# 48 rows for the half tiles, and a new order of the first thousand tasks, in a fused RWKV-7 and MLP kernel

## The chip, the core and the metric

The kernel runs on one core of a Trainium2 chip. A core has a matrix engine (TensorE, PE in the profile, with its weight loads as PEld), a vector engine (VectorE, DVE), a scalar engine (ScalarE, ACT), a general engine (GpSimd, POOL) and a queue engine (SyncE, SP), which here issues every DMA. The engines run side by side, each takes its instructions strictly in order, and semaphores make one wait for another. Matrix products land in PSUM, which has eight banks; everything else lies in SBUF, 128 partitions wide.

The metric is device time in microseconds (us), the median of several executions. Before the change it is 678.03 us (three runs, 677.79 to 678.33).

## The reference

Two stages follow each other. The first is a recurrence over 768 time steps, for 4 batches and 8 heads of size 40:

```python
for t in range(S):
    kt, vt, rt = (k[:, :, t], v[:, :, t], r[:, :, t])
    wt, at, bt = (w[:, :, t], a[:, :, t], b[:, :, t])
    y[:, :, t] = np.einsum('bhd,bhde->bhe', rt, state)
    Sa = np.einsum('bhde,bhe->bhd', state, at)
    state_decay = state * wt[:, :, None, :] - np.einsum('bhd,bhe->bhde', Sa, bt)
    state = state_decay + np.einsum('bhd,bhe->bhde', vt, kt)
```

The second takes y as 3072 tokens of 320 numbers through an MLP: `h = x @ w_in` (320 to 2048), `g = h / (1 + exp(-1.702 h))`, `g @ w_out` (2048 to 320). All is float32.

## The kernel before

**Units and chunks.** The sequence is cut into 12 chunks of 64 steps, and each chunk into two units (two batches each), so there are 24 units, numbered 0 to 23. Inside a unit the recurrence is solved as a triangular system: products between the inputs (`ps_A`, `ps_RV`, `ps_N`), an inverse in five levels of block doubling (`ps_level`), two corner products (`ps_Q`, `ps_T`), the solve (`ps_X`), and the reading of y and of the new state (`ps_y`). Units of the same parity follow each other through the state: `ps_zT` and `ps_rz` bring the state of unit i - 2 into unit i. When both units of a chunk are done, the chunk goes through the MLP: 80 tasks `ps_up`, in eight groups, and after the activation 32 products per group of tokens, `ps_down`.

**The loads (function `load`, line 495).** Per unit five inputs come from DRAM: `ak` (the inputs a and k), `b`, `rv` (r and v), `RV` (v again, in another layout) and `time`. `ak`, `b` and `rv` hold two halves of 64 partitions each, one per half of the heads. A head has 40 channels, so of the 64 partitions of a half only the first 40 carry data. The array in DRAM has all 128 rows, with zeros in the others. The kernel fetches 40 rows of each half, with one DMA per half; the remaining partitions of `ak` and `b` are set to zero once, at the start. `ak` and `rv` have 4 KB per row, `b` 2 KB. Each of these tiles has two buffers, so the load for unit i waits until unit i - 2 has done with its own.

**The weights (function `weight`).** They arrive packed in eight pieces, numbered 0 to 3 for `w_in` and 4 to 7 for `w_out`, in four DMAs of 320 KB each (task name `wt`). Each piece is then unpacked: one step on ACT (`rebased`, line 447), three on DVE (`bounded`, line 451; `shifted`, line 455; `rounded`, line 459) and one on GpSimd (`joined`, line 463).

**One unit's way to y.** `ak` is multiplied on DVE or GpSimd by decay factors (`ahT`, `khT`, lines 619 and 624), `b` on DVE (line 621). `ps_N` needs both. Its masked copy (line 722, into the tile PT) and the transpose of that (line 729, into EX) feed the first level. In the first four units a level is one product of 64x96 blocks and one with an identity; after each, line 792 copies 768 elements per partition from PSUM into PT, and line 729 transposes 512 of them into EX. The next level needs both. The last level's transpose is ES (line 708). Then come `ps_Q`, line 824 or 826 (QT), `ps_T`, line 838 (T), `ps_X`, line 915 (M), `ps_y`, line 953 (y's read-out), and line 961, which makes x from y. x is stored to DRAM and fetched back in another layout (lines 971 and the one after it); both units of a chunk must be back before its first `ps_up`.

**The order.** The work consists of 2700 tasks. `Plan.add` collects them with what each reads, writes and may run on. No scheduler runs in the kernel: the string `ORDER` lists all tasks in the order in which they are issued, each as a number, a letter for its engine (p PE, a ACT, d DVE, g POOL, s SP) and, for tasks that touch PSUM, the number of the pair of banks (0 to 3). So `108a0` is task 108 on ACT with pair 0. `Plan.listed` reads the string, and the tasks are issued one after the other; an engine executes its own in that order.

Of the kernel before, what the change touches and what calls it, by code (L numbers as in the profile page):

```python
# [107 lines left out]
0s 5s 7s 8s 9s 3a 6s 87p0 88p1 24s 89a1 1s 2s 12s 102a 95d 100p2 90a0 93d 158a 101d2 98p3 96g 10s 94d 17s 97g 16s 99d3 103p1  # L108
4a 11s 132p0 104a1 105d1 142p2 26s 143p3 133a0 106d 130p1 14s 144a3 13s 107p0 15s 18s 151g 108a0 109d0 51s 131a1 110p3 27s
149g 150d 111a3 112d3 159p0 156p1 145a2 161d0 160a0 152g 113p3 345s 92a 162d 25s 153d 114a3 163p2 42s 115d3 34s 19a 274s 264p0  # L110
165d2 265p3 164a2 22d 266a3 166p2 20d 273s 21d 33s 43s 167a2 154p3 168d2 23g 35s 28a 157d1 116p2 155d3 169p1 117a2 118d2 267a0
279d 63s 280g 119p3 277s 171d1 36s 44s 120d3 343s 125d3 278g 124d3 29d 126p2 170a1 123a3 30d 172p1 122a3 127a2 121a 31d 128p2
54s 173a1 287a 288p0 289a0 129d2 32g 174d1 134p3 147s 37a 290d0 175p2 135d3 180a2 146s 178a2 275s 176d2 136p1 179a2 479s 38d
181a2 45s 39d 177a 282g 291d 91s 138a1 182p0 188p3 281d 183a0 186p2 139d 137a1 283p0 187a2 184p1 189a3 40d 276s 292p2 46a
284d0 41g 285p3 185d1 344s 148a 286d3 190p0 293a2 294d2 334p1 335p3 357a 140s 191d0 268g 336a3 315d 192p2 47d 337a1 348d 316p0
194a2 295p3 349d 61s 317a0 195g 60s 347s 358p1 296a3 62s 297d3 360d1 318a0 298p3 271a 361d 319p0 338g 300d3 196s 193a2 320a0
346s 355p2 385d 270s 48d 299a3 362p0 356d2 351g 301p3 363a0 364d0 350g 269s 141s 386p2 197s 302d3 365p0 387a2 352g 359a1 303d3
388a2 323p1 367d0 366a0 321p3 49d 324a1 304p2 322a3 478s 325d1 50g 353p0 309a2 470p3 354d0 209p1 307a2 210p1 310a2 305d2 211p1
308a2 272d 198p0 341a 199p0 72s 212p1 70s 64a 200p0 340s 368p2 52s 342d 339s 69s 201p0 369a2 202p0 370d2 203p0 471a 213p1 65d
214p1 389p2 66d 472a3 483g 204p0 390a2 560s 371p3 67d 306a 53s 215p1 71s 482s 216p1 372a3 217p1 476a 220p2 373d3 68g 218p1  # L120
221p2 477d 219a1 205p0 222p2 206p0 223p2 224p2 207p0 55a 311p3 225p2 79s 312d3 80s 226p2 208a0 58d 313p1 374p3 314d1 227p2 56d
379a3 228p2 229p2 57d 326p0 230a2 59g 393p1 327d0 378a3 391p2 394a1 375d3 231p0 558s 392d2 376a 232p0 233p0 395d1 559s 81s 73a
78s 234p0 480s 381p2 235p0 328p1 481s 382a2 74d 377a3 485d 380a3 236p0 75d 492a 242p2 486d 243p2 82a 76d 484d 77g 383p3 237p0
384d3 244p2 329d1 330d1 488p3 473d 238p0 531d 245p2 487g 246p2 489d3 85d 532p1 239p0 533a1 396p3 331d 332s 474s 475s 534a1
240p0 247p2 397d3 562s 241a0 535p1 83d 490p3 536a1 84d 398p0 572a 491d3 86g 550p1 555s 561s 253p3 399d0 551a 333s 400d0 254p3
401d 402s 554s 255p3 552a1 564d 493p0 705s 556a 567g 570p1 403s 494d0 248p2 563d 566g 249p2 495d0 498d 256p3 571d1 565g 250a2
496a0 251d2 252s 696p1 497g 557d 539p0 537p2 704s 257p3 538a2 540d0 258p3 553d 611d 697a 499d 573p2 784s 700s 259p3 576a2
574d2 710d 260p3 541d0 575d2 404p0 578d 261a3 577g 405p0 579d 698a1 568p2 711g 500p1 406p0 569d2 501a1 407p0 262d3 263s 708s
580p2 702a 502d1 408p0 582d2 409p0 503d 410p0 583d 504a 612p3 411p0 584g 613d3 412p0 614d3 413p0 505p1 709d 414a0 426p3 506d1
427p3 428p3 507d1 429p3 699d 581d2 430p3 615p1 785s 706s 701s 703d 431p3 616a1 585p0 432p3 508d 586a0 433p3 587d0 434p3 509a  # L130
588d 435p3 589d 448p2 436a3 510p1 590p0 511a1 449p2 592d0 591a0 512d1 415p3 513d 416p3 593d 514a 417p3 594g 418p3 515p0 419p3
516a0 517d0 595p1 518d 420p3 596a1 597d1 421p3 598d 422p3 519a 599d 423p3 424p3 520p0 425a3 437p1 521d0 438p1 523d0 522g 439p1
524d0 440p1 525d0 441p1 442p1 526d0 527p3 718p0 929s 528a3 443p1 719d0 787s 444p1 720d0 529p3 445p1 721d0 446p1 530d3 600p0
723d 447a1 542p3 722d 724g 603d0 605a0 619p1 604d0 543d3 450p2 620a1 606d0 544p3 621d1 601d0 602d 617p1 707s 546d3 451p2 618a1
783s 712d 547g 713d 607p0 725p1 608a0 452p2 609p0 453p2 548s 610d0 932s 454p2 727d1 726d1 622p0 728d 545d3 729a 775p1 455p2
623d0 780s 776a 549s 756d 730p3 624p0 456d2 457d2 731d3 458s 459p2 777a1 778g 732d3 786s 788g 781a 779s 626d0 460p2 625d0 627g
733d 795p1 835d 734a 461p2 735p3 791g 462p2 628s 736a3 796d1 737d3 716p0 792g 738d 463p2 782d 739g 1011s 920p1 757p3 925s
464p2 717d0 758a3 629s 759a3 790d 465p2 740p0 789d 466p2 741a0 742d0 921a 797p3 467d2 760p0 1008s 468d2 800a3 923d 652p2 469s
761d0 922a1 653p2 926a 930s 798d3 714p1 799d3 654p2 924s 802d 801g 655p2 934d 803a 656p2 836p0 657p2 715d1 658p2 659p2 837d0
762p3 838d0 927d 660p2 763a3 661p2 764p1 662a2 743d 630p0 744d 928s 631p0 632p0 765d1 804p3 766d1 633p0 805a3 806d3 634p0 807d  # L140
635p0 808a 745p2 636p0 748d2 637p0 749d2 839p1 933g 750d2 638p0 840a1 1009s 751d2 639p0 809p3 746d2 935g 640a0 641p1 810d3
642p1 793p2 747a 811d3 674p0 812d 794d2 813a 752p3 643p1 753a3 814p2 644p1 815a2 816d2 754p3 645p1 755d3 646p1 817d 647p1 818a
767p2 841p3 768d2 648p1 842a3 649p1 819p2 650p1 820a2 821d2 675p0 769p3 822d 651a1 823d 771d3 931s 770d3 772g 824p2 936d 676p0
827a2 828a2 942p1 829a2 677p0 1153s 830a2 937d 945a1 773s 663p3 825d2 664p3 943d1 1156s 826a 665p3 944d1 999p2 947d 946g 666p3
1000a 1004s 980d 940p1 948g 667p3 941d1 668p3 774s 669p3 670p3 831p1 671p3 1001a2 1002d 1003s 832d1 672p3 1005a 1013d 678p0
673a3 1006d 833p2 843p1 679p0 834d2 1007s 844d1 938p2 845d1 680p0 939d2 846p3 681p0 847d3 949p1 1012g 682d0 848p2 950a1 683d0
1014d 684s 685p3 849d2 1015g 1010s 850d2 1021p0 1016g 951d1 686p3 1024a0 1232s 851d 1235s 981p2 687p3 982a2 952d 852s 1022d0
983a2 953g 1144p1 1023d0 688p3 1026d 1145a 1149s 1025d 1027g 984p2 1059d 689p3 1154s 954p0 853s 985a2 1147g 690p3 1158d 1148s
955a0 956d0 986p2 1146a1 957d 1150a 691p3 958d 987a2 1151d 988p0 692p3 989a0 1152s 990d0 959p1 693a3 865p2 960a1 694d3 866p2
961d1 867p2 695s 962d 868p2 963d 1028p0 869p2 1029a0 1030d0 870p2 1031d 1157g 871p2 1159d 1032a 1060p3 872p2 873p2 1061a3  # L150
874p2 1062d3 1033p1 875a2 854p0 1035d1 855p0 1036d 856p0 1037d 1063p3 857p0 1064d3 1034a1 858p0 964p2 859p0 965a2 966d2 1038p1
967d 860p0 1039a1 1040d1 861p0 1041d 1017p3 968a 1042g 862p0 1018d3 863p0 969p2 864a0 876p1 970d2 877p1 972d2 971g 1043p3
973d2 878p1 1044a3 974d2 879p1 975d2 880p1 881p1 1045d3 1019p0 1046d 976p2 1047a 882p1 1020d0 1233s 883p1 977a2 1166p3 884p1
1169a3 1167d3 1377s 978p0 885p1 1168d3 898p2 1171d 1170g 886a1 979d0 887p3 1172a 1048p0 991p1 1051a0 888p3 1052a0 992d1 889p3
1053a0 890p3 1054a0 891p3 1049d0 993p1 1050a 1067p0 994d1 1160g 1155s 892p3 1161d 1068a0 893p3 894p3 1069d0 1380s 895p3 1204d
# [982 lines left out]
```

## Time and profile before

| | |
|---|---|
| device time, median of 3 runs | 678.03 us (677.79 to 678.33) |
| profiled execution, span from first to last instruction | 676.5 us |
| granted TensorE clock over the span | 0.994 |
| busy DVE, ACT, POOL | 444.6, 331.6, 175.3 us |
| DMA: bytes read and written | 59.15 and 7.86 MB |
| DMA queue of SP: packets, MB, share of 16 engines | 35136, 67.03, 32.6% |

The profile is that of one execution. Its span is the time from the first instruction to the last; the device time of that execution is not told beside it, and the median of the runs lies 1.5 us above the span. In the lists that follow, a row of the timeline is: start, duration, engine, line, operation, written tile <- read tiles, shapes, count, and in brackets the idle time of the engine before it with what ended it. A row of the groups is: line, engine, operation, tiles, shapes, count | busy time, mean duration in ns | idle time before, by what ended it. A row of the waits is: who <- whom, total, times, longest. "issue" means that the engine waited for nothing that the profile shows. The letter q behind an engine is its instruction queue.

### The profile page before, as it was taken

To read this page: it belongs to the slowest core of one execution; us is meant where nothing else is said; L and a number is where in the kernel's file an instruction comes from. 1 tells how busy PE (TensorE), PEld (TensorE's weight loads), DVE (VectorE), ACT (ScalarE), POOL (GpSimd) and SP (SyncE) were. 2 spreads that over 40 slices of the span, in tenths; PEclk is the share of its full clock that TensorE was granted. 3 is DMA by queue.
4 is the path that set the end of the run, shared out by engine and by line. 5 is a ranking of instruction groups with operands and counts; after the bars stand their busy time and mean duration, and the time that the engine had idled before them with its cause. 6 is when DMAs were issued, how large, how long until landed. Compare 5 with 4: busy or idle time off the path is not lost.

```text
span 676.5 us, 42217 instructions
## 1 busy us (share of the span) xinstructions
PE 648.5 (96%) x19488; PEld 553.4 (82%) x19488; DVE 444.6 (66%) x908; ACT 331.6 (49%) x710; POOL 175.3 (26%) x204
## 2 busy tenths in 40 slices
PE   5768999999999999999999999999999999999997
PEld 5657887987998987788888888798888798798785
DVE  4786787777867667767776587768656766675001
ACT  4676755534564655664545445455454354252110
POOL 6344244224123123123123211322412421300000
PEclk9899999999999999999999999999999999999999
DMA  7983736315314314432404413513412411200200
GB/s 230 300 289 94 232 107 187 103 43 154 108 47 149 93 58 117 121 108 72 118 22 132 141 34 109 156 33 108 140 39 71 122 53 54 61 14 15 61 12 20
DMA packets 35313, 69.74 MB, mean 103 GB/s; under 512 B 5440, under 2 KB 14656, under 8 KB 35136
## 3 DMA queue, kind: packets, MB, share of 16 engines
q1 hardware_dynamic: 35136, 67.03, 32.6%
q8 instruction: 153, 2.51, 1.5%
q14 instruction: 24, 0.20, 0.1%
HBM read 59.15 MB, written 7.86 MB: 99 GB/s over the span
## 4 chain that ended last, share of the span: by engine, by line
PE 93%; DMA 2%; DVE 2%; issue 1%; ACT 1%; DVEq 0%; SPq 0%; ACTq 0%
PE ps_up L300 31%; PE ps_down L300 30%; PE ps_level L300 9%; PE ps_y L300 5%; PE ps_B L300 5%; PE ps_X L300 2%; PE ps_N L300 2%; PE ps_rz L300 2%; PE ps_RV L300 2%; PE ps_A L300 2%; PE ps_zT L300 1%; DMA ak<-in_ak 1%; PE ps_cum L300 1%; PE ps_T L300 1%; DMA b<-in_b 1%
## 5 line engine op out<-in xcount | busy, mean ns | idle before, releaser
L300 PE MATMUL ps_up<-xT_all,w_sb 64*64 64x256 f32 x3840 | 251.0, 377 | 0.8 <-issue 0.4
L300 PE MATMUL ps_down<-w_sb,g 64*64 64x320 f32 x3072 | 237.0, 430 | 0.2 <-ACT zr L877 0.2
L300 PEld LDWEIGHTS ps_up<-xT_all,w_sb 64*64 64x64 f32 x3840 | 170.1, 133 | 15.9 <-issue 1.5
L300 PEld LDWEIGHTS ps_down<-w_sb,g 64*64 64x64 f32 x3072 | 128.0, 133 | 42.8 <-ACT zr L877 0.4
L996 ACT ACTIVATE g<-ps_up 128x1024 f32<-128x1024 f32 x48 | 49.2, 1024 | 45.4 <-PE ps_up L300 45.0
L715 POOL TENSOR_TENSOR EX<-ES,quads 128x512 f32<-128x512 f32 x29 | 38.3, 1322 | 112.7 <-DVE ES L708 74.9
L300 PEld LDWEIGHTS ps_level<-W,EX 64*64 64x64 f32 x2560 | 57.8, 134 | 6.7 <-DVE T L838 0.5
L758 ACT COPY W<-ps_level 128x512 f32<-128x512 f32 (+1 forms) x56 | 29.5, 527 | 67.7 <-PE ps_level L300 65.7
L760 DVE TENSOR_TENSOR E<-two,ps_level 128x256 f32<-128x256 f32 x80 | 33.1, 415 | 34.2 <-ACT W L758 30.1
L300 PE MATMUL ps_level<-W,EX 64*64 64x64 f32 (+1 forms) x2560 | 55.4, 217 | 0.1
L713 ACT ACTIVATE EX<-ES,quads 128x256 f32<-128x256 f32 x80 | 36.3, 501 | 31.0 <-DVE ES L708 30.3
L619 POOL TENSOR_TENSOR ak<-ak,FT 128x512 f32<-128x512 f32 x16 | 20.9, 1305 | 76.6 <-DMA ak<-in_ak 53.4
L708 DVE STREAM_TRANSPOSE ES<-E 128x256 f32<-128x256 f32 x80 | 35.3, 443 | 4.4
L300 PE MATMUL ps_level<-PT,EX 64*64 64x64 f32 (+2 forms) x1280 | 32.8, 235 | 5.1 <-DVE EX L729 3.7
L300 PEld LDWEIGHTS ps_level<-PT,EX 64*64 64x64 f32 x1280 | 30.8, 139 | 8.3 <-DVE EX L729 4.2
L300 PE MATMUL ps_y<-M,bh 64*64 64x104 f32 (+1 forms) x768 | 35.6, 250 | 0.7 <-DVE M L915 0.4
L300 PE MATMUL ps_y<-RV,kh 64*64 64x104 f32 (+1 forms) x768 | 35.6, 251 | 0.0
L899 ACT COPY B<-ps_B 128x416 f32<-128x416 f32 (+1 forms) x34 | 16.6, 492 | 33.4 <-PE ps_B L300 33.2
L300 PEld LDWEIGHTS ps_y<-RV,kh 64*64 64x64 f32 x768 | 28.3, 137 | 2.6 <-DVE M L915 0.5
L689 DVE COPY_PREDICATED PT<-within,ps_N 128x256 f32<-128x256 uint32 x40 | 17.8, 444 | 18.5 <-ACT P L697 13.5
L915 DVE TENSOR_TENSOR M<-ps_X,later 128x832 f32<-128x832 f32 (+1 forms) x24 | 23.8, 993 | 8.3 <-PE ps_X L300 8.1
L300 PE MATMUL ps_B<-RV,A 64*64 64x104 f32 (+1 forms) x768 | 27.9, 252 | 1.1 <-issue 1.1
(131 smaller groups left out, 1088.2 us busy)
## 6 DMA issues: line engine op xcount, KB each, us to landing
ak<-in_ak SPq DMA_DIRECT2D x48, 160.0 KB
rv<-in_rv SPq DMA_DIRECT2D x48, 160.0 KB
time<-in_time SPq DMA_DIRECT2D x24, 320.0 KB
xT_all<-x_dram SPq DMA_DIRECT2D x48, 160.0 KB
wc<-in_wc SPq DMA_DIRECT2D x20, 264.0 KB
logw<-in_w SPq DMA_DIRECT2D x24, 160.0 KB
RV<-in_v SPq DMA_DIRECT2D x24, 160.0 KB
b<-in_b SPq DMA_DIRECT2D x48, 80.0 KB
```

Of the source, the lines that this page charges most:

```text
L300: nc.tensor.matmul(o, lhsT, rhs, start=start, stop=True, skip_group_check=True)
L619: plan.add(R, {"DVE": 690.0, "POOL": 1270.0, "sbuf": True}, lambda t: of(t.engine).tensor_mul(ahT(), ahT(), FT_of(i)), reads=T("ak", "FT") ...
L689: plan.add(R, dve(256), lambda t, n=n: nc.vector.copy_predicated(tiles_of(at(E0_t, i)), every(within_of(n), [128, 2, 4, 32]), blocks(psum( ...
L708: plan.add(rank, dve(256), lambda t: nc.vector.transpose(ES(n), source(t)), writes=[key("ES", n, 6)], **reads)
L713: nc.scalar.activation(dst[:, :, h], ES(n), ACT.Copy, scale=quads[:, h, :1])
L715: of(t.engine).tensor_mul(dst, ES(n).unsqueeze(2).to_broadcast([128, 8, 2, 32]), quads.unsqueeze(1).to_broadcast([128, 8, 2, 32]))
L758: plan.add(rank, any2(512 - 8 * past), lambda t: copy(t.engine)(tiles_of(W(n + 1))[:, :, :, past:], blocks(psum(t, ""), 64)[:, :, :, past: ...
L760: plan.add(rank, dve(256), lambda t: nc.vector.tensor_sub(tiles_of(E(n + 1)), every(two32, [128, 2, 4, 32]), blocks(psum(t, ""), 64)[:, :, ...
L899: plan.add(R, any2(4 * wide), lambda t: copy(t.engine)(dst(), some(psum(t, "")[:, :, :208])), writes=[("Bv", i)] if x and c > 0 else T("B" ...
L915: plan.add(R + 1, dve(8 * wide), lambda t: nc.vector.tensor_tensor(M_of(i)[:, :, :wide].rearrange("p (j b) n -> p b j n", b=2), some(psum( ...
L996: plan.add(-45, {"ACT": 1030.0, "table": "gelu"}, lambda t: nc.scalar.activation(g_of(c * NQ + q).rearrange("p m r n -> p r m n"), psum(t, ...
```

## The change

Two things are changed.

1. `load` fetches 48 rows of each half of `ak`, `b` and `rv` in place of 40. The eight rows more are zeros in DRAM and fall on partitions that were zero or unused. Each load has the same number of DMAs as before.
2. The first 1000 of the 2700 entries of `ORDER` stand in another order, with other engines and other pairs of PSUM banks. They are the same 1000 tasks. The other 1700 stand as they did, on the same engines.

```diff
@@ ORDER @@
-0s 5s 7s 8s 9s 3a 6s 87p0 88p1 24s 89a1 1s 2s 12s 102a 95d 100p2 90a0 93d 158a 101d2 98p3 96g 10s 94d 17s 97g 16s 99d3 103p1
-4a 11s 132p0 104a1 105d1 142p2 26s 143p3 133a0 106d 130p1 14s 144a3 13s 107p0 15s 18s 151g 108a0 109d0 51s 131a1 110p3 27s
...
+0s 3a 87p3 7s 158a 88p1 100p0 102a 89a1 5s 8s 1s 4a 101d0 9s 93d 95d 6s 94d 11s 10s 90a3 98p2 97d 103p1 18s 143p3 96g
+17s 99d2 105d1 104a1 142p2 16s 2s 144a3 149g 145a2 106d 107p0 108d0 274s 130p1 92a 151g 15s 109d0 150d 131a1 110p3 112d3
...
@@ -263,6 +270,7 @@
     PLAIN = 4
+    ROWS = 48
     PARTS = 4
@@ -495,7 +503,7 @@
     def load(i):
         for name, of, src, n in (("ak", ak_of, ak_d, 1024), ("b", b_of, b_d, 512), ("rv", rv_of, rv_d, 1024),
                                  ("RV", RV_of, v_d, 320), ("time", time_of, time_d, 2 * DM)):
-            rows = [slice(p.start, p.start + D) for p in HALF] if name in ("ak", "b", "rv") else [slice(0, 128)]
+            rows = [slice(p.start, p.start + ROWS) for p in HALF] if name in ("ak", "b", "rv") else [slice(0, 128)]
```

Read with the names of the tasks, the new order differs from the old one in these places:

| | before | after |
|---|---|---|
| first issues of SP | logw 0, ak 0, rv 0, RV 0, time 0, b 0, a weight piece, logw 1, logw 2, rv 1, ak 1 | logw 0, rv 0, ak 0, RV 0, logw 1, time 0, b 0, b 1, ak 1, three weight pieces, logw 2 |
| weight DMAs issued ahead of `ak` of unit 2 | 11 | 4 |
| weight DMAs issued ahead of the fetch of chunk 0's first x | 22 | 15 |
| `RV` of unit 2 on SP | behind 42 other loads and stores | behind 34, and ahead of `ak` of unit 3 and of unit 0's x store |
| copies at line 792 in units 0 to 3 | 15 on ACT, 1 on DVE | 6 on ACT, 10 on DVE |
| x of unit 0 (line 961) | DVE | POOL |
| join of weight 0 on POOL | ahead of unit 2's `khT` and `ahT` | between them |
| tasks on ACT, DVE, POOL in all | 433, 785, 134 | 405, 800, 147 |

The order of PE's tasks changes little: of its first 55 tasks, 53 stand in both, and the first `ps_up` is the 56th in both.

More of the change, by code (lines that the diff above doesn't have):

```diff
@@ new lines @@
+1744p2 1846a0 1579d1 1581p3 1911g 1847d0 1580s 1746d2 1906s 1880p1 1912g 1745d2 1582p3 2050s 1747d 2131s 1917p0 1583p3
+1848d 1748s 1920a0 1955d 1849g 2128s 1918d0 2040p2 1584p3 1919d0 2041a 2045s 1922d 1921d 1585p3 1923g 1881d1 2042a2
+2044s 2046a 1850p0 2043d 2054d 1586p3 1851a0 1749s 2047d 1884p2 1587p3 1885a2 1852d0 1853d 1882p1 1886d2 1854a 1588p3
+1883d1 2048s 1855p0 1589d3 1750p2 1856a0 1590d3 1751p2 1857d0 1913p1 1591s 1858d 1752p2 1914d1 1753p2 1859a 1754p2
+1924p3 2053d 2055g 1755p2 1925a3 1756p2 1926d3 1757p2 1927d 1915p0 1928a 1758p2 1916d0 1759p2 1860p1 1760a2 1761p3
@@ L245 @@
+2654p1 2679p3 2655a1 2656p0 2657p0 2658p0 2659p0 2660p0 2661p0 2662p0 2663p0 2664p0 2665p0 2680p3 2666a0 2667p2 2668p2
+2669p2 2670p2 2671p2 2672p2 2673p2 2674p2 2675p2 2676p2 2681p3 2677a2 2682p3 2683p3 2684p3 2685p3 2689p1 2686d3 2687d3
+2690p1 2688s 2691p1 2692p1 2693p1 2694p1 2695p1 2696p1 2697d1 2698d1 2699s
 """
```

269 lines of the change are left out of this document (134 added, 135 removed).

## The prediction

> **What bounds the kernel now.** Read first: the page's head, its slices and its queues.
>
> ```profile
> span 676.5 us, 42217 instructions
> PE 648.5 (96%) x19488; PEld 553.4 (82%) x19488; DVE 444.6 (66%) x908; ACT 331.6 (49%) x710; POOL 175.3 (26%) x204
> ...
> PE   5768999999999999999999999999999999999997
> ...
> DMA packets 35313, 69.74 MB, mean 103 GB/s; under 512 B 5440, under 2 KB 14656, under 8 KB 35136
> ```
>
> PE is busy for all but 28.0 us, and the gaps stand in the first four slices and the last one. The busy time by window (time, then busy time of PE, weight loads, DVE, ACT and POOL, granted clock, DMA share, GB/s) places them:
>
> ```profile
> 0.00:17.00 17.00, 9.45 (x248) 8.70 (x248) 8.07 (x14) 7.50 (x26) 10.64 (x43) 1.00 0.77 230
> 17.00:34.00 17.00, 12.31 (x448) 10.75 (x452) 12.47 (x22) 10.80 (x23) 6.79 (x6) 0.90 0.90 301
> 34.00:51.00 17.00, 10.80 (x441) 9.35 (x431) 15.07 (x24) 12.20 (x33) 8.08 (x5) 0.98 0.88 284
> 51.00:68.00 17.00, 14.16 (x607) 13.16 (x606) 10.38 (x17) 11.40 (x31) 7.72 (x9) 0.92 0.33 96
> ...
> 85.00:240.00 155.00, 154.57 (x4723) 134.37 (x4717) 115.86 (x239) 83.72 (x175) 48.33 (x45) 1.00 0.36 108
> 240.00:640.00 400.00, 399.76 (x12146) 337.46 (x12142) 267.26 (x574) 189.25 (x398) 89.52 (x97) 1.00 0.28 83
> ```
>
> Idle before 68 us is 7.55 + 4.69 + 6.20 + 2.84 = 21.3 us; from 85 to 640 it is 0.7; the other 6 are the stretch between and the tail, which the change leaves alone. PE's work is the same in both kernels, so the change can only alter those 21.3 us, or open gaps in the 155 us whose order is also new. The two largest of PE's waits up to 86 us:
>
> ```profile
> PE ps_level L300 <- DVE EX L729: 3.7, 3, 1.7
> PE ps_cum L300 <- POOL logw L367: 3.7, 1, 3.7
> ```
>
> The second is the start-up and stays. All others are links of one chain: inputs, the inverses of the first two units, their outputs y, the round trip of x through DRAM, the first `ps_up`. Its marks on the timeline:
>
> ```profile
> 6.68 0.69 DVE L624 TENSOR_TENSOR ak<-ak,GT 128x512 f32<-128x512 f32 x1 [2.00 <-ACT GT L565]
> 7.00 0.47 PE L300 MATMUL ps_RV<-rv 40*64 40x64 f32 x2 [1.65 <-DMA rv<-in_rv]
> 8.01 1.02 PE L300 MATMUL ps_RV<-rv 40*64 40x64 f32 x27 [0.53 <-DMA rv<-in_rv]
> 10.25 0.78 DVE L621 SCALAR_TENSOR_TENSOR b<-b,GT 128x512 f32<-128x512 f32 x1 [0.29 <-DMA b<-in_b]
> 11.29 1.14 PE L300 MATMUL ps_N<-b,ak 40*64 40x64 f32 x32 [1.30 <-DVE b L621]
> 13.21 0.69 DVE L722 TENSOR_TENSOR PT<-ps_N,within 128x512 f32<-128x512 f32 x1 [1.57 <-ACT P L697]
> 14.95 1.43 PE L300 MATMUL ps_level<-PT,EX 64*64 64x96 f32 x32
> ...
> 32.61 0.41 DVE L708 STREAM_TRANSPOSE ES<-ps_level 128x256 f32<-128x256 f32 x1
> 39.00 1.02 DVE L915 TENSOR_TENSOR M<-ps_X,later 128x832 f32<-128x832 f32 x1
> 42.81 0.58 ACT L953 COPY zr<-ps_y 128x512 f32<-128x512 f32 x1
> 50.21 0.51 PE L300 MATMUL ps_cum<-logw,edges 64*64 64x160 f32 x3 [2.13 <-issue]
> 53.82 0.42 PE L300 MATMUL ps_y<-M,bh 64*64 64x104 f32 x8
> 67.55 1.89 PE L300 MATMUL ps_up<-xT_all,w_sb 64*64 64x256 f32 x29
> ```
>
> From 67.55 on `ps_up` fills every gap. So the question is when the new order reaches its first `ps_up`.
>
> **The rows.** Of 412 issues, those of `ak`, `b`, `rv` and the store of x have 40 rows, 192 in all:
>
> ```profile
> ak<-in_ak SPq DMA_DIRECT2D x48, 160.0 KB
> rv<-in_rv SPq DMA_DIRECT2D x48, 160.0 KB
> ...
> b<-in_b SPq DMA_DIRECT2D x48, 80.0 KB
> ...
> x_dram<-x SPq DMA_DIRECT2D x48, 80.0 KB
> ```
>
> The 5440 small packets of the page are 220 x 16 + 192 x 10: a 40-row transfer closes on ten DMA engines, any other on 16. [...] From the rows: the two halves of `rv` released PE 1.0 us apart. The window from 17 to 34 moved 301 GB/s at a share of 0.90, 334 when full, so 192 KB over all engines take 0.6; if the rows themselves set the pace, a half takes 1.2. I take 0.6: the small packets name ten busy engines, not the rows, as what is short. Per half of `ak` or `rv` that is 0.4 gained (0.2 lost at worst), per half of `b` half of it. Later on, a fifth more bytes in these loads fall into a DMA share of 0.28 to 0.36 and cost nothing; without that cover, 0.1 a half.
>
> **The order, first link.** `b` of unit 0 held N until 11.29. The new SP order is rv, ak, RV, logw of unit 1, time, b. Up to b's end stand four halves (-1.6), b's own two (-0.4) and one new 160 KB logw (+0.5): b lands 1.5 earlier, at about 8.7; at worst 1.5 later. DVE first does `RV`, `ahT` and `khT` (0.7 each, from 6.7) and is free at 8.8. So N starts at 9.7, not 11.29; and `PT`, now ahead of ACT's `P`, no longer waits 1.57 for it: the first level starts at 12.4, not 14.95.
>
> **The levels.** Groups up to 85 us, and a level on the chain of waits:
>
> ```profile
> L729 DVE STREAM_TRANSPOSE EX<-ps_level 128x512 f32<-128x512 f32 x16 | 11.3, 710 | 12.6 <-ACT PT L792 12.2 <-PE ps_level L300 0.3
> L792 ACT COPY PT<-ps_level 128x768 f32<-128x768 f32 x12 | 9.6, 797 | 7.4 <-PE ps_level L300 4.4 <-DVE EX L729 2.2 <-ACT wch L569 0.7
> L447 ACT ACTIVATE w_sb<-extra 128x1280 f32<-128x1280 f32 x3 | 4.2, 1407 | 0.7 <-DMA x_dram<-x 0.7
> L638 DVE TENSOR_TENSOR A<-ps_A,upper 128x512 f32<-128x512 f32 x4 | 2.7, 684 | 1.8 <-PE ps_A L300 1.8
> L961 POOL TENSOR_TENSOR x<-zr,FT 128x128 f32<-128x128 f32 x4 | 1.7, 456 | 6.6 <-ACT zr L953 6.6
> ...
> 57.22 1.11 PE ps_level L300 x40
> ```
>
> DVE's transpose sat 12.2 us behind ACT's copy of the same bank. Ten of these copies move to DVE. A 768-element copy on DVE is not in the trace: between `A` (512, 0.68) and `M` (832, 1.02), so 0.92, near `M` by size. A level then costs 1.11 + 0.92 + 0.71 and 0.15 of handing over, 2.9; ACT's 0.80 gave 2.8. The copy is 0.1 dearer; what is won is that ACT's weight steps (1.4 each) no longer stand ahead of it, which is why five levels of unit 0 took from 14.95 to 32.61. I followed the new order link by link, each task starting once its engine's last one and its inputs are done, with these durations: the last level ends at 28.0 (five levels in 15.6, not 17.7), M of unit 0 starts at 32.8 (39.00) and its read-out at 36.0 (42.81). The x product of unit 0 moves to GpSimd, 1.7 for 0.9: its store has until unit 1's x, so it is covered; uncovered, 0.8.
>
> **To the first up.** From there to the end of unit 1's y: 7.6, not 11.4, of which 2.13 was a wait at `ps_cum` that nothing in the profile explains; so 43.6, not 54.24. From y to the first `ps_up`: 14.4, not 13.3, since DVE now has the copies of two units, with 13.1 of PE work in it. The up starts at 58.0 with 0.6 more PE work done: 9.5 + 0.6 = 10.1 us gained.
>
> SP now stands at unit 2's `RV` until unit 0's y is read, some 7 us; behind it wait unit 3's `ak`, a weight piece and the x store. They land by 39 to 42, and the first user (`ahT`, 43) comes later. Unit 1's x product ends at 47.2; its round trip, at most 67.55 - 56.7 = 10.9 (GpSimd's x product ended 56.7), is back by 58.1: just covered, and each us on it beyond costs one.
>
> **Charges.** GpSimd against DVE, on the timeline:
>
> ```profile
> 26.17 0.82 DVE L451 TENSOR_SCALAR w_sb<-w_sb 128x1280 f32<-128x1280 f32 x1
> 33.80 1.26 POOL L619 TENSOR_TENSOR ak<-ak,FT 128x512 f32<-128x512 f32 x1
> 34.01 1.74 DVE L451 TENSOR_SCALAR w_sb<-w_sb 128x1280 f32<-128x1280 f32 x1
> 37.42 2.97 POOL L463 TENSOR_TENSOR w_sb<-w_sb 128x1280 int32<-128x1280 int32 x1 [2.36 <-DVE w_sb L459]
> ```
>
> One operation took 0.82 alone and 1.74 beside GpSimd, ending 0.7 after it: it was held until GpSimd was done. In the new order the 2.97 us join of weight 0 falls at 29.8 to 32.8, and unit 2's `b` product, ahead of `T` on DVE, is due at 30.4: 0 to 2.4 us on the chain, taken in full, as in that row. Weight steps beside the next joins: 0 to 0.9, taken as 0.5. The unexplained wait may come again, 0 to 2.1: 1.0. Together 3.9.
>
> [...]
>
> **Sum.** 10.1 - 3.9 = 6.2: a span of 670.3. The profiled span lies 1.5 below the median of 678.0; with that, 671.8. Under 0.2% (1.4 us) a change cannot be told from none.
>
> **Rivals.**
> 1. No charge falls due: 10.1 and up to 12, about 667. For it: with `RV` holding SP, the queue is emptier when instructions are fetched. Against: the 1.74.
> 2. It does not do what it says. A 48-row half takes 1.2, b lands at 10.2 + 1.5 and N 3.0 later than in my chain; and the 3.8 of the link between the two y come back, as PE waits there on other inputs: 10.1 - 3.0 - 3.8 - 3.9 = -0.6, about 678.6. Against: ten engines in the packet count.
> 3. Slower. In the first thousand tasks ACT gives up 28, DVE gains 15 and GpSimd 13: at their groups' means +11 us on DVE and +16 on GpSimd. DVE, 115.9 of 155 us from 85 to 240, goes towards 80%, and meets GpSimd more often. A held operation loses 0.92 (1.74 - 0.82). Where it feeds PE without slack, PE stops. From seven such stops on, the gain is gone; ten give 9.2 - 6.2 = 3 us slower, 681. For it: PE idles 0.4 us there now, so any stop is new. Against: `ps_up` and `ps_down` stand between the links there.
>
> **How the numbers follow.** Forecast (3 to 8 us gained) 0.48; rival 1, 0.22; rival 2, 0.08; rival 3, 0.22. Faster 0.70, same 0.08, slower 0.22. The forecast's own range is 670 to 675; the wide one goes to 665.5 for rival 1's end and to 681 for rival 3.
>
> **What would show it.** In the changed profile: small packets 5440 + 144 x 6 = 6304 (the rows); N near 9.7, the first `ps_up` between 58 and 62, idle before it 11 to 15 (the chain); a DVE product over 1.3 us beside the first join near 30 to 33 (the charge); 85 to 240 with under 1 us of PE idle (against rival 3). The forecast is wrong if `ps_up` starts after 65, or if the idle comes back after it.

## The result, and the profile after it

The changed kernel takes 707.06 us (median of four runs, 705.73 to 712.32); the kernel before, on the same chip, 677.91. The ratio is 1.0441, 95% interval 1.0397 to 1.0485: 29 us slower, where 6 us faster was forecast.

The page of the changed kernel, its head and slices. `load` and all lines behind the string stand 8 lines lower than in the profile of before (line 619 is now 627).

```profile
span 704.2 us, 42184 instructions
PE 661.2 (94%) x19488; PEld 558.7 (79%) x19488; DVE 465.8 (66%) x920; ACT 309.8 (44%) x669; POOL 194.7 (28%) x223
...
PE   5776888999999999999999999999999999999997
...
DMA packets 37328, 73.66 MB, mean 105 GB/s; under 512 B 6304, under 2 KB 15520, under 8 KB 37152
...
q8 instruction: 153, 2.51, 1.5%
```

The span grew by 27.7 us. PE, with the same 19488 products, was busy 12.7 us longer (661.2 for 648.5) and idle 15.0 us longer (43.0 for 28.0). The busy time by window (same columns as in the prediction: span, PE, weight loads, DVE, ACT, POOL, granted clock, DMA share, GB/s) says where:

```profile
0.00:17.00 17.00, 8.90 (x229) 7.76 (x231) 10.04 (x18) 7.38 (x26) 10.31 (x43) 1.00 0.93 267
17.00:34.00 17.00, 12.21 (x400) 11.49 (x392) 12.20 (x17) 6.24 (x17) 3.43 (x3) 0.90 1.04 297
34.00:51.00 17.00, 12.48 (x503) 11.62 (x495) 14.30 (x23) 8.38 (x25) 10.17 (x9) 0.90 0.31 85
51.00:68.00 17.00, 12.59 (x500) 11.70 (x504) 10.59 (x15) 7.22 (x22) 7.78 (x9) 0.90 0.83 256
68.00:85.00 17.00, 14.65 (x371) 12.04 (x360) 15.12 (x19) 10.07 (x21) 8.69 (x4) 0.90 0.56 174
85.00:120.00 35.00, 26.64 (x604) 20.09 (x608) 31.82 (x42) 15.06 (x27) 20.25 (x11) 0.80 0.56 159
...
85.00:240.00 155.00, 145.09 (x4196) 121.79 (x4200) 114.19 (x220) 65.66 (x136) 55.52 (x52) 0.96 0.38 105
240.00:640.00 400.00, 395.84 (x12161) 336.16 (x12156) 279.75 (x591) 196.97 (x411) 98.76 (x104) 1.00 0.34 93
```

Two things are to be seen. Up to 85 us PE idles 24.2 us, hardly more than the 22.5 of before. From 85 to 240 it idles 9.9 where it had 0.4, nearly all of it (8.4) before 120, where DVE is busy 31.8 of 35 us; from 240 to 640, 4.2 for 0.2. And the granted clock is lower: four windows of 17 us at 0.90 and one of 35 at 0.80 are some 27 us at half clock up to 120, against 6.8 in the windows of before (0.90, 0.98, 0.92). PE was busy for 24.8 of them, and for all 6.8 before; half of the difference, 9.0 us, is an estimate of what this makes of PE's 12.7 us more.

The marks of the chain on the timeline after, in order of time:

```profile
9.55 0.89 DVE L629 SCALAR_TENSOR_TENSOR b<-b,GT 128x512 f32<-128x512 f32 x1 [0.89 <-DMA b<-in_b]
10.70 1.14 PE L308 MATMUL ps_N<-b,ak 40*64 40x64 f32 x32 [0.85 <-DVE b L629]
13.41 1.56 PE L308 MATMUL ps_level<-PT,EX 64*64 64x96 f32 x32 [0.18 <-DVE EX L737]
34.58 0.45 DVE L716 STREAM_TRANSPOSE ES<-ps_level 128x256 f32<-128x256 f32 x1 [0.30 <-PE ps_level L308]
36.33 2.94 POOL L471 TENSOR_TENSOR w_sb<-w_sb,extra 128x1280 int32<-128x1280 int32 x1
36.72 3.10 DVE L629 SCALAR_TENSOR_TENSOR b<-b,GT 128x512 f32<-128x512 f32 x1
40.03 0.72 PE L308 MATMUL ps_N<-b,ak 40*64 40x64 f32 x32 [2.24 <-POOL w_sb L471]
42.19 1.02 DVE L923 TENSOR_TENSOR M<-ps_X,later 128x832 f32<-128x832 f32 x1 [1.22 <-PE ps_X L308]
45.93 0.59 ACT L961 COPY zr<-ps_y 128x512 f32<-128x512 f32 x1
53.76 0.40 PE L308 MATMUL ps_y<-M,bh 64*64 64x104 f32 x8
74.32 1.04 PE L308 MATMUL ps_up<-xT_all,w_sb 64*64 64x256 f32 x12
```

The chain starts earlier than before (N at 10.70, not 11.29; the first level at 13.41, not 14.95), is level with it at the end of unit 1's y (54.16, before 54.24) and reaches its first `ps_up` 6.8 us later.

**PE waits for its own instructions.** PE's largest waits without a releaser ("issue") up to that point:

```profile
16.67 0.78 PE L308 MATMUL ps_B<-RV,A 64*64 64x104 f32 x10 [0.94 <-issue]
23.01 0.31 PE L308 MATMUL ps_level<-PT,EX 64*64 64x96 f32 x3 [1.09 <-issue]
29.31 0.34 PE L308 MATMUL ps_level<-PT,ident 64*64 64x128 f32 x4 [2.11 <-issue]
51.78 0.62 PE L308 MATMUL ps_cumc<-edges,logw 64*64 64x65 f32 x26 [2.17 <-issue]
55.51 0.27 PE L308 MATMUL ps_zT<-ident,zr 40*40 40x40 f32 x4 [1.09 <-issue]
60.71 0.36 PE L308 MATMUL ps_zT<-ident,zr 40*40 40x40 f32 x15 [2.02 <-issue]
70.44 0.25 PE L308 MATMUL ps_B<-RV,A 64*64 64x104 f32 x1 [2.08 <-issue]
```

They end in the middle of a task, whose first products ran before the wait, so none of its inputs can be the cause. Counted over PE's stream (weight loads, products, semaphore instructions), they end at the indices below. Beside them stands the packet on the instruction queue (q8, whose packets are all of 16384 bytes) that landed last, and how long after its start and its end PE went on:

```
PE goes on   index   modulo 256   packet            from its start   from its end
16.67          448      192       14.25 - 15.39         2.42             1.28
23.01          703      191       20.32 - 21.55         2.68             1.45
29.31          959      191       26.82 - 28.03         2.49             1.28
51.78         2240      192       48.87 - 50.24         2.91             1.54
55.51         2496      192       52.95 - 54.26         2.56             1.25
60.71         2751      191       58.03 - 59.28         2.68             1.42
70.44         3263      191       67.59 - 69.30         2.86             1.14
```

So PE's instructions come in lines of 256, one a packet: the trace has 153 such packets for 39268 instructions of PE, 257 each. PE stands still where a line ends before the next is there; I call these stops fetch waits. The unexplained 2.13 us of before, at 50.21, is one of them: index 2239, 1.31 after a packet landed.

**The clock falls after a thin window.** Windows of 3.41 us of the changed kernel, in pairs that follow each other (columns as above):

```profile
26.87:30.28 3.41, 1.30 (x60) 1.17 (x53) 2.24 (x2) 0.40 (x3) 1.09 (x1) 1.00 1.03 353
30.28:33.69 3.41, 3.38 (x94) 3.28 (x87) 2.44 (x5) 0.37 (x1) 0.00 (x0) 0.51 1.04 330
...
67.83:71.24 3.41, 1.33 (x69) 1.13 (x63) 2.53 (x4) 0.11 (x1) 0.79 (x1) 1.00 0.59 209
71.24:74.65 3.41, 3.41 (x101) 3.37 (x97) 2.45 (x4) 2.94 (x5) 2.18 (x1) 0.51 0.56 154
84.89:88.31 3.42, 0.93 (x48) 0.79 (x48) 3.39 (x2) 3.42 (x5) 2.46 (x1) 1.00 1.04 309
88.31:91.72 3.41, 2.14 (x48) 1.83 (x52) 2.67 (x7) 1.14 (x1) 2.69 (x1) 0.51 0.36 71
91.72:95.13 3.41, 3.41 (x56) 2.62 (x52) 3.40 (x5) 1.09 (x6) 1.54 (x2) 0.50 0.68 181
```

A window with 0.9 to 1.3 us of PE work is followed by one at half clock, and where that one again isn't full (2.14), by a second. The changed kernel has eight such stretches of 3.41 us up to 120 us, the kernel before two.

The column has no entry before 20.1 us after the change, and none before 16.1 in the kernel before; the windows count that as 1.00. The pace of a level's 32 products says otherwise. It is the same at 13.41 as at 31.52, which is at half clock, and not that of 26.25, at full clock:

```profile
26.25 0.89 PE L308 MATMUL ps_level<-PT,EX 64*64 64x96 f32 x32 [1.02 <-DVE PT L800]
31.52 1.56 PE L308 MATMUL ps_level<-PT,EX 64*64 64x96 f32 x32
```

By this pace PE ran at half clock up to the column's first entry. It was busy for 12.0 us until then, for 9.0 in the kernel before; half of the difference is 1.5 us more of the 12.7, again an estimate. The other 2.2 were not taken apart.

**What stands behind DVE from 74 us on.** The operations of DVE and GpSimd that lie side by side there, and PE's waits that follow:

```profile
83.89 3.47 POOL L471 TENSOR_TENSOR w_sb<-w_sb 128x1280 int32<-128x1280 int32 x1 [2.83 <-DVE w_sb L463]
84.47 3.57 DVE L459 TENSOR_SCALAR w_sb<-w_sb 128x1280 f32<-128x1280 f32 x1
88.82 0.71 DVE L737 STREAM_TRANSPOSE EX<-ps_level 128x512 f32<-128x512 f32 x1
89.58 1.08 PE L308 MATMUL ps_level<-PT,EX 64*64 64x32 f32 x32 [2.86 <-DVE EX L737]
97.92 3.34 POOL L471 TENSOR_TENSOR w_sb<-w_sb,xT_all 128x1280 int32<-128x1280 int32 x1 [4.66 <-DVE xT_all L467]
98.36 3.58 DVE L463 TENSOR_SCALAR w_sb<-w_sb 128x1280 int32<-128x1280 int32 x1
103.07 0.59 PE L308 MATMUL ps_B<-RV,A 64*64 64x104 f32 x16 [1.03 <-DVE QT L834]
107.50 4.72 DVE L969 TENSOR_TENSOR x<-zr,FT 128x128 f32<-128x128 f32 x4
108.68 2.98 POOL L471 TENSOR_TENSOR w_sb<-w_sb,extra 128x1280 int32<-128x1280 int32 x1
113.53 0.71 PE L308 MATMUL ps_T<-QT,Tc 64*64 64x64 f32 x16 [3.47 <-DVE P L707]
```

A weight step that took 0.82 alone in the kernel before takes 3.57 here beside a join of 3.47 and ends 0.7 after it; the links behind it on DVE come late, and PE stands for 2.86, 1.03 and 3.47 us: 7.4 of its 8.4 idle us there. DVE has four operations of over 3 us up to 130 us, each beside a join; in the kernel before it has none.

### The profile page after: what moved, and what is told of

The parts are those of the page before. It is cut to its first block, busy times and chain, and to the rows that moved or that the text cites. A ratio compares the mean times of both kernels' runs of the same rounds, so it can differ in the third digit from the quotient of the medians.

```text
span 704.2 us, 42184 instructions
## 1 busy us (share of the span) xinstructions
PE 661.2 (94%) x19488; PEld 558.7 (79%) x19488; DVE 465.8 (66%) x920; ACT 309.8 (44%) x669; POOL 194.7 (28%) x223
## 2 busy tenths in 40 slices
DMA packets 37328, 73.66 MB, mean 105 GB/s; under 512 B 6304, under 2 KB 15520, under 8 KB 37152
## 4 chain that ended last, share of the span: by engine, by line
PE 86%; DVE 5%; issue 4%; DMA 2%; POOL 1%; ACT 1%; SPq 0%; DVEq 0%; POOLq 0%; ACTq 0%
PE ps_down L308 29%; PE ps_up L308 27%; PE ps_level L308 9%; PE ps_B L308 5%; PE ps_y L308 5%; PE ps_X L308 3%; PE ps_N L308 2%; PE ps_rz L308 1%; PE ps_RV L308 1%; PE ps_A L308 1%; PE ps_zT L308 1%; POOL w_sb L471 1%; PE ps_T L308 1%; PE ps_cum L308 1%; PE ps_Q L308 1%
## 5 line engine op out<-in xcount | busy, mean ns | idle before, releaser
L308 PE MATMUL ps_down<-w_sb,g 64*64 64x320 f32 x3072 | 240.1, 433 | 0.2 <-ACT zr L885 0.2
L308 PEld LDWEIGHTS ps_up<-xT_all,w_sb 64*64 64x64 f32 x3840 | 166.6, 134 | 21.4 <-issue 2.2
L308 PEld LDWEIGHTS ps_down<-w_sb,g 64*64 64x64 f32 x3072 | 133.1, 134 | 42.4 <-issue 2.3
L723 POOL TENSOR_TENSOR EX<-ES,quads 128x512 f32<-128x512 f32 x34 | 45.0, 1325 | 123.4 <-DVE ES L716 87.4
L766 ACT COPY W<-ps_level 128x512 f32<-128x512 f32 (+1 forms) x48 | 25.5, 532 | 66.2 <-PE ps_level L308 56.6
L627 POOL TENSOR_TENSOR ak<-ak,FT 128x512 f32<-128x512 f32 x17 | 23.7, 1395 | 70.4 <-DMA ak<-in_ak 40.2
L308 PE MATMUL ps_level<-PT,EX 64*64 64x64 f32 (+2 forms) x1280 | 36.3, 249 | 6.5 <-DVE EX L737 3.0
L308 PEld LDWEIGHTS ps_level<-PT,EX 64*64 64x64 f32 x1280 | 33.6, 151 | 10.2 <-DVE EX L737 3.7
L635 POOL TENSOR_TENSOR kh<-time,G 128x320 f32<-128x320 f32 x19 | 16.9, 891 | 50.5 <-PE ps_y L308 30.8
L308 PEld LDWEIGHTS ps_B<-RV,A 64*64 64x64 f32 x768 | 25.9, 140 | 6.2 <-issue 1.6
```

What stands on the lines that cost most here:

```text
L308: nc.tensor.matmul(o, lhsT, rhs, start=start, stop=True, skip_group_check=True)
L627: plan.add(R, {"DVE": 690.0, "POOL": 1270.0, "sbuf": True}, lambda t: of(t.engine).tensor_mul(ahT(), ahT(), FT_of(i)), reads=T("ak", "FT") ...
L635: plan.add(R + 4, {"POOL": 870.0, "DVE": 490.0, "sbuf": True}, lambda t, n=n, dst=dst: of(t.engine).tensor_mul(dst(i)[:, :, :D], by_head(t ...
L723: of(t.engine).tensor_mul(dst, ES(n).unsqueeze(2).to_broadcast([128, 8, 2, 32]), quads.unsqueeze(1).to_broadcast([128, 8, 2, 32]))
L766: plan.add(rank, any2(512 - 8 * past), lambda t: copy(t.engine)(tiles_of(W(n + 1))[:, :, :, past:], blocks(psum(t, ""), 64)[:, :, :, past: ...
```

## The experiments

The kernel before had a median of 680.1 to 682.1 in the later runs, so each ratio is taken on its own chip. A fetch wait is as above; the sums of waits and of half clock are in us. The table has for 14 of the 17 profiles the start of the first `ps_up`, what stood before it (fetch waits, PE's other idle time, time shown at half clock, each stretch where it starts), and the last two from there to 130 us. It is worked out from the traces, one execution each, so differences of a us or two can be chance:

```
profile                  first up  fetch  other  half clock | to 130: other  half clock
before                     67.6     4.7   16.6      6.8     |          0.2      0.0
rows48_old_order           69.0     3.2   17.0     13.7     |          0.2      0.0
old_lines_64               71.8     8.2   16.3      6.8     |          0.2      0.0
old_lines_128              70.3     8.6   14.4      6.8     |          0.2      0.0
old_order_new_engines      70.5     2.2   20.2     13.7     |          1.4      0.0
old_until_up               73.9     8.8   14.7     13.7     |          4.5      6.8
after                      74.3    11.9   12.0     13.6     |          8.6     13.7
rows40_new_order           76.4    13.5   14.3     17.1     |          8.0     10.2
changed_again              78.7    15.3   11.9     23.9     |          8.4     13.7
lines_shifted              78.2    13.3   12.4     20.5     |          9.0     13.7
new_lines_128              74.6    11.6   10.1     30.7     |          9.5     13.7
holds_moved                76.9    18.0    9.8     17.1     |          8.5      3.4
gap_filled                 78.3    13.8   12.9     23.9     |          3.9      3.4
new_order_old_engines      74.6     9.9   13.9     20.5     |         10.3      6.8
```

**The rows and the order apart.** First the old order with 48 rows:

```diff
-slice(p.start, p.start + D)
+slice(p.start, p.start + 48)
```

> The order of before with 48 rows in place of 40: the rows alone. Theory O (the loss is the order's and its engines'): within 2 us of before (677.9), as 96 more packets on six more engines cost little; PE busy 647 to 650. Theory R (48 rows fill all 16 DMA engines, and what PE fetches through them, its instructions, comes late): 4 to 12 us slower than before, with PE's waits that have no releaser ('issue') up to 75 us summing to 10 us or more, in place of 5.8. Theory C (the clock): the kernel's PE busy time exceeds 640 us by half of the time at half clock, so each new stretch of 3.4 us at half clock adds 1.7 us.

Ratio 1.0051 (1.0019 to 1.0083): 3.5 us slower, with 3.2 us of fetch waits, not more than before. Its page shows a longer busy time, at a granted clock of 0.988 for 0.994:

```profile
span 680.8 us, 42217 instructions
PE 654.0 (96%) x19488; PEld 552.6 (81%) x19488; DVE 446.8 (66%) x908; ACT 332.5 (49%) x710; POOL 175.8 (26%) x204
```

5.5 us more than the 648.5 of before for the same products. Then the new order with 40 rows:

```diff
-    ROWS = 48
+    ROWS = 40
```

> The new order with 40 rows: the order alone. Theory O: 704 to 710, as the changed kernel (707.1). Theory R: 695 to 701, and 'issue' waits of PE up to 75 us back at 4 to 6 us from about 12. If both O and R hold a part, the two runs with one part each add up to the 29 us: (rows alone) + (order alone) = 29 within 3. Theory C: as for the other, six stretches of half clock where the gaps stay, fewer where they go.

Ratio 1.042 (1.0377 to 1.0463), as with 48 rows, and 13.5 us of fetch waits. So the order, with its engines, makes the loss, and the theory that 48 rows delay PE's instructions falls: with 40 rows they are as late. The rows are worth half a percent in the old order, in the wrong direction, and nothing that shows in the new one.

**The order and the engines apart.** Every task of the new order on the engine that it had, and the reverse (one token of 120 shown):

```diff
-... 108d0 ...
+... 108a0 ...
```

> The changed kernel, with the tasks in the new order and each of the 120 tasks whose engine differs put back on the engine that it had before (ACT again has 433, DVE 785, POOL 134). Theory E (the loss is the work moved from ACT to DVE and GpSimd, where the joins hold DVE): the idle of PE between 85 and 120 us falls from 8.4 to under 3 us, and the time to 688 to 697. Theory S (the loss is the order, first of all on SP, which stands at the RV of unit 2 from 31 to 45 us): first ps_up still later than 72 us, 700 to 708.

> Before, with the order of before and 40 rows, but each of the 120 tasks on the engine that it has in the changed kernel. Theory E: slower than before by 10 us or more, 688 to 700, with PE idle between 85 and 120 us above 3 us. Theory S: 676 to 682, as the order of the work and of the DMAs is untouched.

1.067 (1.0603 to 1.0738) and 1.0187 (1.0153 to 1.0222). The first is a miss for both theories: the new order with the old engines is worse still. Perhaps the order of each engine's work fits only the engines that it was made for; no run shows it. The second was foreseen by theory E in its size, 691.3, but PE's idle from 85 to 120 us is 0.7, not 3: the new engines cost 2% in the old order, in other places. The two parts don't add up and can't be priced apart.

**SP's sequence.** In these, only SP's tokens stand in the other order's sequence:

```diff
-0s 7s 5s 8s 1s 9s 6s 11s 10s 18s 17s 16s 2s 274s ...
+0s 5s 7s 8s 9s 6s 24s 1s 2s 12s 10s 17s 16s 11s ...
```

> The new order and engines with 40 rows (706.9 in its run), but SP issues its DMAs in the sequence of before. Four fetches that the new order's first units need early (logw 3 and three more) are taken forward. Theory S (SP's sequence is the cause: RV of unit 2 holds SP with an empty queue for 14 us, and what stands behind it comes late): 682 to 692, first ps_up near 67. Theory L (the order of the links on DVE, ACT and GpSimd before the first ps_up): 698 to 708 with the first ps_up still after 71. Theory U (the order from the first ps_up on): also 698 to 708, and PE idle between 85 and 120 us stays above 5 us.

> The order and engines of before with 40 rows, but SP issues in the sequence of the changed kernel (ten issues that would otherwise be waited for in a circle are taken forward). Theory S: 693 to 708. Theories L and U: within 3 us of before (676 to 683); the fetch of b ahead of the first weights even starts N0 of unit 0 0.5 to 1.5 us sooner than 11.29.

1.0715 (1.0648 to 1.0782) and 1.0637 (1.0553 to 1.0722), with the first `ps_up` at 84.7 and 84.4. Both orders lose with the other's sequence: in the first, PE waits 8.6 us for one N behind GpSimd's `ak` and 9.2 for `rv`; in the second, 9.7 for one `ps_cum` behind `logw`, none of which the changed kernel has. The times, 728.84 and 722.49, lie outside what any of the theories said. That SP's hold at unit 2's `RV` (31 to 45 us) is the cause by itself is neither shown nor excluded.

**The two halves.** The new order up to the first `ps_up` and the old one behind it, and the reverse; tasks without a free pair of banks at the seam are put off (the first list goes on where it says):

```diff
-<the new order's first 243 tasks, then the new order>
+<the new order's first 243 tasks, then the old order's other tasks>
```

> 40 rows. The tasks up to the first ps_up in the new order (243 of them, on the new engines), all others in the order and on the engines of before. Theory L: first ps_up after 71 us and 688 to 700, with PE idle from 85 to 120 under 3 us. Theory U: 677 to 686, as little more is lost than what the first ps_up is late by. Theory S: 690 to 706, as SP's hold lies in this part.

> 40 rows. The tasks up to the first ps_up in the order of before (257 of them), all others in the new order and on the new engines. Theory L and S: 676 to 686, first ps_up near 67.5. Theory U: 692 to 706, with PE idle from 85 to 120 us above 5 us and at least one stretch of half clock there.

1.0268 (1.0207 to 1.0329) and 1.0278 (1.0194 to 1.0362). Both mixtures lose. The first figure has the seam in it: PE waits 8.0 us there at a `ps_cum` behind DVE, which neither order has. Up to the seam PE is as late as in the changed kernel: the last product ahead of it starts at 74.2 us in both. In the second, PE's first 1712 products are the old order's very tasks, and yet they are done only at 70.8, not 67.5, with 7.2 us of fetch waits where before had 4.7, and twice its half clock: the same list of PE's tasks isn't met by the same waits each time. Two tasks of PE that the new order puts ahead follow, and the first `ps_up` comes at 73.9. From 85 to 120 PE idles 4.5 us (theory U said over 5), and two stretches of half clock came, as it said.

**The changed kernel again, and three edits of it, on one chip.** The kernel as it is:

> The changed kernel as it is, on the same chip as the three edits of it that follow. 704 to 713 on every theory. In its profile: the waits of PE with no releaser again end at those instructions of PE whose index is 191 or 192 modulo 256, 1.1 to 1.6 us after a packet of 16 KB on the instruction queue has landed (theory F: PE waits for its own instructions), and 10 us or more of them up to the first ps_up. Every stretch of 3.41 us in which PE is busy less than 1.7 us is followed by one or two such stretches at half clock (theory C).

714.75 us, 1.0481 (1.0441 to 1.052). All its eight fetch waits over 1 us end at 191 or 192 modulo 256, 1.3 to 1.5 us after a packet. From the clock column's first entry on, each window under 1.7 us was followed by half clock, as theory C has it. Then the tasks beside joins moved (one of the moves; the two lists differ by seven tasks moved):

```diff
-... 121g ... 23g 176d3 ...
+... 23g 121g ... 176d3 ...
```

> The changed kernel with nine tasks moved in the order, none to another engine: the join of weight 0 ahead of the first spread, so that it does not lie beside unit 2's b product; the sums of chunk 4 ahead of weight 3's steps; the third step and the join of weight 2 behind weight 5's steps; unit 4's b product and the step of weight 6 ahead of weight 4's last step; x of unit 2 right behind its y. Theory H (joins on GpSimd hold DVE operations of two SBUF inputs or of 1280 elements for 2.9 to 3.6 us, and PE's gaps between 85 and 120 us are what stands behind them): the operations of more than 3 us on DVE up to 120 us fall from 4 to 1 or none, PE's idle between 85 and 120 us from 8.4 to under 4 us, and the time to 694 to 702. Without H: within 3 us of the changed kernel.

709.0, 1.039 (1.0339 to 1.044): 5.8 us less. The window from 85 to 120, of the changed kernel again and of this one:

```profile
85.00:120.00 35.00, 26.56 (x624) 20.31 (x620) 33.83 (x43) 16.50 (x28) 19.42 (x10) 0.86 0.59 170
```

```profile
85.00:120.00 35.00, 28.06 (x699) 21.18 (x694) 34.23 (x47) 15.61 (x28) 20.27 (x12) 0.95 0.64 188
```

Idle fell from 8.4 to 6.9 only, not under 4; what came was the clock, 0.95 for 0.86. Of DVE operations over 3 us one is left of four, but the joins hold others in their place: in windows of half a microsecond a single operation fills DVE from 92.5 to 95.0, 102.5 to 104.0 and 113.0 to 115.0, with GpSimd busy for 5.7 of these 6.0 us. DVE is busy 34.2 of 35 us, so any neighbour of a join is on its way. From the first `ps_up` to the same product later (15,500 before the last) it takes 89.9 us, not 94.7. Theory H said under 4 us of idle and a time of 694 to 702, and neither came. Without H the time was to stay within 3 us, and it fell by 5.8. So its share is too large; that joins hold DVE and DVE holds PE is read from the rows above, and this run alone doesn't prove it.

More work in the gaps:

```diff
-            for b, f in product(BITS, BITS):
+            for _, b, f in product(range(5 if i == 3 else 1), BITS, BITS):
...
-                for v, f in product(BITS, BITS):
+                for v, f in product((0,) * (6 if i == 3 and x == 0 else 0) + BITS, BITS):
```

> The changed kernel with more work and nothing taken away: PE makes ps_A of unit 3 five times in place of once, and the first part of one ps_B of unit 3 seven times, 256 and 192 instructions of PE more, just ahead of the two gaps at 86.7 and 110 us. The result is the same. Theory C (a window of 3.41 us with under 1.7 us of PE work is followed by half clock): the gaps are filled, the two double stretches of half clock behind them go, and although PE has 6 us more to do, the time is 2 to 6 us shorter, 700 to 705. Without C: 0 to 6 us longer.

718.1, 1.0533 (1.0493 to 1.0573): not faster, a miss in the time. In its profile three of the four stretches of half clock between the first `ps_up` and 130 are gone, and from there to the same later product it takes 92.1 us for 94.7, with 224 products more. The one stretch that is left follows a fetch wait of 3.1 us: the 256 instructions of the filling brought a line's end into it. So the filling keeps the clock, and this one execution doesn't say more: it is the fastest of its kernel's four (714.6), and that of the changed kernel again the slowest (717.0).

The lines shifted by 64 instructions:

```diff
-            for e, b in product(BITS, BITS):
+            for _, e, b in product(range(2 if i == 0 else 1), BITS, BITS):
```

> The changed kernel with ps_RV of unit 0 made twice: 64 instructions of PE more, at 6.5 us, where PE waits. Theory F: each wait with no releaser still ends at an index of 191 or 192 modulo 256, so it moves to another task, 64 instructions earlier in the program; their sum up to the first ps_up changes by 2 us or more either way, and the time with it. If the waits belonged to the tasks (a PSUM bank, an input that the trace does not show), they would stay at the same products: the third level of unit 1, ps_cumc of chunk 3, ps_zT of units 2 and 3 and ps_B of unit 2, and the time within 2 us.

724.1, 1.0599 (1.0535 to 1.0663). All eight waits of over 0.6 us again end at 191 or 192 modulo 256 (959, 1215, 1471, 2240, 2496, 2751, 3008, 3263), that is, 64 instructions earlier in the program, and so at other products. They belong to the line's end and not to a task. Their sum is 13.3 us, 2.0 less than in the changed kernel again, and yet the 64 instructions in a gap cost 9.4 us. About 3 of them are clock (44.4 us at half clock up to 640, for 37.5), the rest wasn't taken apart.

**Where the lines fall, or the order.** The same edit in the old order, and with `range(3 ...)` in both:

> Before (old order, 40 rows), with ps_RV of unit 0 made twice: 64 instructions of PE more near 8 us, where PE waits for b; so all lines of 256 fall 64 instructions earlier in the program. Position theory (the waits depend on where the lines fall): their sum up to the first ps_up, 2 to 5 us in most runs of the old order, becomes 8 or more, and the time 4 to 10 us longer than before. Order theory (they belong to the new order's denser chain): the sum stays at 2 to 6 us and the time within 4 us of before.

> The same with ps_RV of unit 0 made three times: 128 instructions more, a shift by half a line; N of unit 0 starts 1.1 us later for it. Position theory: the waits come where they were rarest, a sum of 8 us or more up to the first ps_up, 5 to 12 us slower than before. Order theory: a sum of 2 to 6 us, 0 to 5 us slower.

> The changed kernel with ps_RV of unit 0 made three times: a shift by half a line, N of unit 0 1.2 us later. Position theory: the waits fall to half in one of the two shifts of the new order; since the shift by 64 kept them at 13 us, here 4 to 8 us, and the time is below the changed kernel's. Order theory: again 12 to 18 us of them, the time 0 to 10 us above the changed kernel's.

1.0061 (1.004 to 1.0081), 1.0115 (1.0073 to 1.0157) and 1.0478 (1.0438 to 1.0519). In the old order the waits rose from 4.7 to 8.2 and 8.6 us and the time with them: the lines of the old order lie well, and a shift spoils it. In the new order they were 11.9 to 15.3 unshifted, 13.3 and 11.6 shifted: no shift tried takes it below. So both theories hold a part, as far as one profile of each can say: some 4 us are where the lines fall, the rest comes with the new order.

## Why the prediction was wrong, step by step

1. **The rows** came as said: 6304 small packets, so a 48-row half has 16 of them where a 40-row half had ten. That a 48-row half takes 0.6 us over 16 DMA engines was the author's estimate, and no run shows it: in the changed trace the 4 KB packets of the first four halves of `rv` and `ak` go from 2.35 to 6.10, 0.94 a half, and in that of before, with 40 rows, from 3.14 to 7.10, 0.99 a half. That they bring `b` early came in part: it landed at 9.45, 0.8 earlier than the 10.22 of before, not 1.5, and N started at 10.70, not 9.7.
2. **PT ahead of P** held: the wait of 1.57 is gone. The first level started at 13.41, not 12.4; the 1.0 is N's.
3. **The levels** failed: 15.6 us forecast, 21.6 measured (13.41 to 35.03, the end of ES). The copy on DVE was sized right, 0.92 us. Three fetch waits (0.94, 1.09, 2.11), 4.1 us in all, fall into this stretch; the clock is at half from 30.3 to 33.7, and by the pace of the products also up to 20.1, where before it rose at 16.1.
4. **The charge of the first join** came true: `bhT2` took 3.10 beside the join, held 2.4 us as charged; it is the 2.24 us of PE's wait at 40.03.
5. **From the read-out to y's end** held: 8.2 us (45.93 to 54.16) for 7.6. **To the first up** failed: 20.2 us, not 14.4; 5.2 of it are fetch waits (1.09, 2.02, 2.08), and two stretches of half clock lie in it. The round trip of x did not decide: it was back at 67.05, 7 us before its use.
6. **SP's hold at `RV`** was 14 us (31 to 45.4), not 7. The joins that followed at 28 to 107 us before now lie at 36 to 121, among the links of units 2 to 5.
7. **The term that failed first** is the charge "The unexplained wait may come again, 0 to 2.1: 1.0". It was no single wait but PE's supply of instructions at every 256th of them. What I forecast for PE's waits on other engines came about: 16.6 before, 12.0 after, 4.6 less (the prediction had 11 to 15 for all idle time). The fetch waits rose by 7.2 (4.7 to 11.9), and half clock by 6.8 us, worth up to 3.4. Together that is 6.0 later, of the 6.8 measured; the half clock at the start and the 32 products more that PE has ahead of the first `ps_up` (1744 for 1712) are not in this sum. Nothing in the link-by-link sum could take time back when a link got shorter; PE's instructions and its clock did, and for the clock the prediction had no term.
8. **"From 67.55 on `ps_up` fills every gap"** failed for the new order. Rival 3 had the right mechanism and place, with 0.22 and at most 3 us; its price was mis-sized: 0.92 us a held operation, from one row, where those that stop PE lost 2.8 each (3.57 and 3.58 less 0.82), and 85 to 240 idles 9.9 us and not under 1. It also had no term for what follows a gap: from 85 to 120 PE is busy for 11.2 us at half clock, which costs some 5.6 us more.
9. Both signs named as fatal came: `ps_up` after 65, and idle after it.

Of the 27.7 us, 6.8 lie before the first `ps_up`. The product 12,000 before PE's last, past the reordered tasks, starts 24.3 us later (285.3 for 261.0); the last 3.4 arise in tasks whose order is the same, on other banks. A fetch wait of 1.7 us at 412.5 is among them; no run here took the rest apart. No experiment points to a kernel that beats the one before.

Open: why the new order's fetch waits are longer. In the seven cases above the next line's packet starts when PE has some 10 to 140 of the last line's 256 instructions left, so a wait shortly before a line's end does not always hide the fetch; what starts it, the traces don't show. Open too is the half percent of the 48 rows.

## What to carry to other kernels

Before adding up gains on a chain of small products, list the waits that have no releaser with their index in PE's stream; where they sit on a modulus, as 102 of 103 here at 190 to 193 modulo 256, look at the supply of instructions: the chain that was to be shorter had 11.9 us of them for 4.7. Where a gap left PE at most 1.75 us of work in a window of 3.41, half clock followed in 74 of 78 cases; add it, by estimate 1.7 us for one such stretch and 3.4 for two. A work split moved towards GpSimd is priced by its longest instructions beside DVE's, at their full length, not by one average row: here 3.57 and 3.58 us for 0.82, beside joins of 3.47 and 3.34.

## What the runs showed of the hardware

- **Instructions.** In 17 profiles, of 113 gaps of PE over 0.6 us up to 130 us that end at 190 to 193 modulo 256, 105 end 1.1 to 1.8 us after an instruction packet of 16 KB landed; the packet's start lies 2.2 to 2.9 us before PE goes on in nine of ten. Of the 103 gaps of this size that have no releaser, 102 end at such an index. About half of PE's instructions are products (19488 of 39268), some 128 a line, and the 1712 products before the first `ps_up` took 46.5 us of PE's time in the kernel before, 27 ns each or 3.5 us a line: by this estimate the 2.2 to 2.9 us from a packet's start are most of a line's time.
- **Clock.** In the same profiles up to 600 us, on each one's grid of 3.41 us: 79 windows at full clock were followed by half clock, 74 of them with at most 1.75 us of PE work; of 2635 followed by full clock, 4 had so little. Half clock ended only after a window with 2.84 us or more. So a window busy for up to half of its time was enough. The entries of the clock at half speed up to 600 us last 3.41 or 6.83 us in the traces of before and of the changed kernel.
- **The clock's column starts late.** N of unit 0 takes 1.14 us at 10.70 and N of unit 2 0.72 at 40.03, both under a column of 1.00: before its first entry the column does not show half clock.
- **Spread.** The kernel before went from 676.6 to 685.5 us over the chips, the changed one from 704.5 to 717.0 with either number of rows. The grid of 3.41 us lies elsewhere in each run; whether that makes the spread was not tried.
